# Clustered attention with two MLPs: late transposes ahead of score tiles, key penalties undivided, two roundings as SyncE copies, and a new order of the first units

## The chip, the cores and the metric

The kernel runs on one core of a Trainium2 chip. The metric is the time of one execution on the device in microseconds (us), as the median of several runs. The core's engines are TensorE (PE; its weight loads are listed apart as PEld), VectorE (DVE), ScalarE (ACT), GpSimd (POOL) and SyncE (SP), which in this kernel issues the DMAs.

## The reference

Eight heads of two batches attend within clusters: a query sees only the keys whose nearest centroid is its own. The result goes through two MLPs.

```python
q_assign = argmax(einsum('bhsd,hcd->bhsc', q_n, c_n))      # S = 768, D = 64, 16 clusters
k_assign = argmax(einsum('bhsd,hcd->bhsc', k_n, c_n))
mask = q_assign[:, :, :, None] == k_assign[:, :, None, :]
scores = where(mask, scale * q @ k.T, -1e9)
attn_out = softmax(scores) @ v                              # B = 2, H = 8
x = attn_out as (1536, 512)
h = maximum(maximum(x @ w1, x @ w2), x @ w3); x = h @ w_out         # d_ff = 768
h = x @ w_in; g = maximum(0.01 * h, h); out = g @ w_out             # d_ff = 2048
```

## The kernel before

**Work.** Heads go in eight pairs; a pair fills 128 partitions with 2 x 64 dimensions. A unit is one head of a pair and a group of 256 queries, so that a pair has six units and the attention 48 (n = 0 to 47). In the first pair the units are (0,0), (0,1), (1,0), (1,1), (0,2), (1,2) as (head, group); in later pairs an even unit is head 0 and an odd one head 1. Each value is kept as a rounded part and a rest (fp32r), which gives operands q1, q2, k1, k2 per head and for even and odd pairs: `k1_0_1` is k1 of even pairs, head 1. Sixteen rows of q2 and k2 hold one-hot clusters and penalties (`oo`), by which keys of other clusters fall out of the softmax.

**Operations of a unit n.** S0:n and S1:n are score tiles of 128 queries by 768 keys (PE, L659, four matmuls: a first half from q1 and k1, a second half from q2 and k2, which needs the penalties); SA and SB are these halves apart. M0, M1 are the maxima (VectorE, L665), X0, X1 the exponentials (ScalarE, L671, tile `ee`), R the inverse of their sums, Q0, Q1 the normalising (GpSimd, L685). T0, T2, T4 transpose two of six blocks of both halves (PE, L692, four transposes each); E0, E2, E4 bring them out of PSUM (L705, L707, tile `et`). V is the product with the values for two units (PE, L716, 24 matmuls), Y its store into `acc` (ScalarE, L722).

**Operations of a pair p.** G, C, H are the cluster similarities (L545, L553, L561), Na, Nb, W, FA, FB the one-hot of the first nearest cluster; O and P are its transposes (PE, L578) and the penalties (ScalarE, L583, tile `oo`). QH, QL, KH, KL round and take rests. D*@p copies operands into their places by SyncE's queue: Dq, Dk, Dl, Dm those of queries, keys and rests (64x768, 192 KB each), Da and Db the penalties of head 0 and of head 1 (four copies of 16x384, 24 KB). LD and LV load a pair's queries and keys (2 x 384 KB) and values. F fetches MLP weights (`raw` and `low`, some 512 KB each); I3 and I2 are idle matmuls on zeros (L836). The first pair has operations of its own: Gq, Gk, Naq to FBk as above for queries and keys apart, UQ and UK the transposes of the query and the key one-hots (L532), CQ and CK the query and key penalties out of PSUM, and Z.. the roundings of head a and b: `Zbr` fills q2 of head 1, `Zbj` the lower half of k1 of head 1 (ScalarE, L419), `Zbm` is GpSimd's rest for k2 of head 1, which reads that lower half. `Hd` is a small cast on GpSimd (`hold`), by which its work begins when the first one-hots are there.

**Order.** Each engine works through its instructions in the order of the program, and waits only for semaphores. That order is written out by hand: BEGIN lists the operations of units 0 to 14 and what goes with them, ORDER has one row for each of the six units of a pair (the number behind / or + is an offset in units or pairs) and serves the rest, and END ends the attention. ONCE names operations that are done once, ahead of a given one, and skipped where they would have come. What stands ahead of another on an engine, and on SyncE's queue, is read from these.

A piece of the operand copies, where Da and Db are:

```python
elif part == "ab"[j]:
    for b in range(4):
        rows = slice((2 * b + j) * C, (2 * b + j + 1) * C)
        cols = slice(b % 2 * HALF, (b % 2 + 1) * HALF)
        dma((q2, k2)[b // 2][D : D + C, cols], s["oo"][rows])
```

Of the kernel before, what the change touches and what calls it, by code (L numbers as in the profile page):

```python
# [8 lines left out]
F32 = mybir.dt.float32  # L9
F32R = mybir.dt.float32r  # L10
BF16 = mybir.dt.bfloat16
AF = mybir.ActivationFunctionType
# [34 lines left out]
)  # L47

BEGIN = (
    "Gq Zaq Zal Zak Naq Nbq Zaj Gk Wq Zbj FAq Zbq Nak SA0:0 FBq Zar Nbk I3 UQ Wk CQ FAk SA1:0 G@1 Zbk FBk UK  "  # L50
# [14 lines left out]
)  # L65
AFTER = 12

END = "h h V:47 h h Y:47"

ONCE = {  # L70
    "V:43": "in x0 x1 x2 x3", "T0:46": "ph h h", "T4:46": "h h", "T0:47": "h", "T4:47": "h h",
    "E4:47": "oh",
}
# [15 lines left out]
def clustered_attention_mlps(  # L89
# [229 lines left out]
    with ExitStack() as att:  # L319
# [302 lines left out]
        def first_operands(j, what):  # L622
            s = st[0]
            q1, q2, k1, k2 = opnd[0][j]
            rq, rk = (s[x][j * D : (j + 1) * D] for x in ("rq", "rk"))
            if what == "q":
                rounded("A", q1[0:D], rq, SCALE)
            elif what == "r":
                rounded("A", q2[0:D], rq, SCALE)
            elif what == "k":  # L630
                rounded("A", k1[0:D], rk)
            elif what == "j":
                rounded("A", k1[D:P], rk)
            elif what == "l":
                rest("D", q1[D:P], rq, q1[0:D], SCALE)
            else:
                rest("DP"[j], k2[0:D], rk, k1[j * D : (j + 1) * D])
# [91 lines left out]
        def scrap(key):  # L729
            if key not in scraps:  # L730
                scraps[key] = small_bank()
            return scraps[key]
# [82 lines left out]
        if True:  # L815
# [65 lines left out]
            def start(op):  # L881

                if op[0] == "I":
                    idle(int(op[1:]))
                elif op[0] == "Z":
                    first_operands("ab".index(op[1]), op[2])
                elif op == "Hd":

                    nc.gpsimd.tensor_copy(hold, oh0[:, D + 2 * C : D + 2 * C + 1])
                elif op == "Ct":  # L890
                    end_third()
                elif op == "D2":
                    operands(0, "2")
                elif op == "w":
                    take_apart()
                elif op in ("Gq", "Gk"):
                    sims(0, "qk".index(op[1]), scrap(op))
                elif op in ("Naq", "Nak"):
                    near_max(0, "qk".index(op[2]), scrap("G" + op[2]))
                elif op in ("Nbq", "Nbk"):  # L900
                    near_eq(0, "qk".index(op[2]))
                elif op in ("Wq", "Wk"):
                    weigh(0, nc.vector, "qk".index(op[1]))
                elif op in ("FAq", "FAk"):
                    first_max(0, "qk".index(op[2]))
                elif op in ("FBq", "FBk"):
                    first_eq(0, "qk".index(op[2]))
                elif op in ("UQ", "UK"):
                    onehot_up(0, "QK".index(op[1]), scrap(op))
                elif op == "CQ":  # L910
                    ps = scrap("UQ").bitcast(BF16)[D : D + C, 0:S]
                    nc.scalar.copy(opnd[0][0][1][D : D + C], ps)
                elif op in ("CK", "CL"):
                    up = slice(D, D + C)
                    cols = slice(0, HALF) if op == "CK" else slice(HALF, S)
                    ps, out_ = scrap("UK").bitcast(BF16)[up, cols], opnd[0][0][3][up, cols]
                    if op == "CK":
                        nc.scalar.activation(
                            out_, ps, AF.Identity, scale=gain[up], bias=base[up]
                        )  # L920
                    else:
                        nc.vector.tensor_scalar(
                            out_, ps, gain[up], base[up], op0=ALU.mult, op1=ALU.add
                        )
                elif op == "OT":
                    for h in range(2):
                        onehot_T(0, h, scrap(op)[:, 256 * h : 256 * h + 256])
                elif op == "PA":
                    penalties(0, scrap("OT"))
                elif op == "in":  # L930
                    until_scores.close()
                    open_inputs()
                elif op == "oh":
                    until_transposes.close()
                    open_hidden()
                elif op == "F":
                    fetch_pieces()
                elif op == "ph":
                    until_exps.close()
                    open_products()  # L940
                    st["first"] = hidden(0, 0)
                elif op == "h":
                    next(st["first"])
                elif op[0] == "x":
                    split_x(0, (int(op[1]),))
                else:
                    raise ValueError(op)
# [109 lines left out]
```

## Time and profile before

| | us |
|---|---|
| three runs | 695.46, 695.75, 698.95 |
| median | 695.75 |
| profiled execution, own time | 696.57 |
| its span | 694.8 |

The span runs from the first to the last instruction of the profiled execution; the own time holds some 1.8 us around it. In the rows below a group of instructions stands with its line, engine, operation and tile; "x4" is how many are taken together; what stands in square brackets is idle time of the engine just ahead and what ended it. Line numbers of the kernel after the change are one to five higher.

### The profile page before, as it was taken

The numbers are of one execution on the slowest core, as the hardware profiler recorded it, in microseconds if no ns is written. First come the engines' busy times: TensorE is split into PE (matmuls) and PEld (weight loads), VectorE is DVE, ScalarE is ACT, GpSimd is POOL, SyncE is SP. The second block draws the span as 40 slices with busy tenths as digits, with TensorE's granted clock in tenths as the row PEclk, the third lists the DMA queues.
The fourth block names the chain that finished last, engine by engine and source line by source line (L and its number), as shares of the span: only waits on it lengthen the run. The fifth ranks groups of instructions, "written<-read, shape, count | busy, mean of one in ns | idle before, by whom it ended". The sixth has DMA issues, their size and how long they took to land.

```text
span 694.8 us, 10351 instructions
## 1 busy us (share of the span) xinstructions
PE 684.9 (99%) x3715; PEld 551.0 (79%) x3717; DVE 489.0 (70%) x896; ACT 336.9 (48%) x635; POOL 217.7 (31%) x201
## 2 busy tenths in 40 slices
PE   8999999999999999999999999999999999999997
PEld 5677778777786788888888888888888888888886
DVE  6887788888867398788783798797359847972222
ACT  6877777877877354323231344454434324431120
POOL 4855456465544011011111102322322223312220
PEclk9999999999999999999999999999999999999999
DMA  3969748427401166545541344265215522500102
GB/s 120 235 153 268 196 112 242 136 74 200 101 13 50 51 204 204 173 157 162 169 161 52 121 152 152 62 204 189 91 54 188 166 77 91 182 30 1 57 34 91
DMA packets 30083, 89.96 MB, mean 129 GB/s; under 512 B 4785, under 2 KB 5681, under 8 KB 30033
## 3 DMA queue, kind: packets, MB, share of 16 engines
q1 hardware_dynamic: 30032, 89.32, 42.7%
q8 instruction: 29, 0.48, 0.3%
q14 instruction: 22, 0.17, 0.1%
HBM read 68.16 MB, written 3.15 MB: 103 GB/s over the span
## 4 chain that ended last, share of the span: by engine, by line
PE 94%; DMA 2%; POOL 1%; DVE 1%; ACT 1%; issue 0%; SPq 0%; ACTq 0%; POOLq 0%
PE h L246 13%; PE h L247 13%; PE h L248 13%; PE o L716 9%; PE s L659 9%; PE y L246 9%; PE y L248 9%; PE y L247 9%; PE t L692 8%; DMA k<-kh 1%; PE s L836 1%; DMA k<-oo 1%; PE t L545 1%; DVE xl L237 1%; ACT ee L671 0%; PE t L465 0%
## 5 line engine op out<-in xcount | busy, mean ns | idle before, releaser
L280 POOL TENSOR_TENSOR hl<-a,hh 128x512 fp32r<-128x512 f32 x66 | 92.0, 1394 | 355.5 <-ACT hh L279 355.5
L246 PE MATMUL h<-xh,wh 128*128 128x512 f32 x408 | 159.3, 390 | 0.0
L248 PE MATMUL h<-xh,wl 128*128 128x512 f32 x408 | 158.8, 389 | 0.0
L247 PE MATMUL h<-xl,wh 128*128 128x512 f32 x408 | 158.7, 389 | 0.0
L665 DVE TENSOR_REDUCE mx<-s 128x1 f32<-128x768 f32 x96 | 90.8, 954 | 36.1 <-PE s L659 27.5
L685 POOL TENSOR_SCALAR ee<-ee,rs 128x768 f32<-128x768 f32 x96 | 90.5, 956 | 62.0 <-DVE rs L680 34.9
L246 PE MATMUL y<-hh,wh 128*128 128x512 f32 x264 | 102.7, 389 | 0.0
L247 PE MATMUL y<-hl,wh 128*128 128x512 f32 x264 | 102.7, 389 | 0.0
L248 PE MATMUL y<-hh,wl 128*128 128x512 f32 x264 | 102.7, 389 | 0.0
L279 ACT CAST hh<-a 128x512 fp32r<-128x512 f32 x66 | 41.1, 623 | 126.3 <-DVE a L273 75.4
L659 PE MATMUL s<-k,q 128*128 128x512 f32 (+3 forms) x384 | 93.0, 363 | 3.2 <-ACT ee L671 1.6
L671 ACT ACTIVATE ee<-s,mx 128x768 f32<-128x768 f32 x96 | 86.8, 905 | 19.1 <-DVE mx L665 15.3
L246 PEld LDWEIGHTS h<-xh,wh 128*128 128x128 f32 x408 | 76.6, 188 | 16.5 <-issue 0.8
L248 PEld LDWEIGHTS h<-xh,wl 128*128 128x128 f32 x408 | 76.6, 188 | 16.0
L247 PEld LDWEIGHTS h<-xl,wh 128*128 128x128 f32 x408 | 76.6, 188 | 15.6
L271 ACT COPY a<-h 128x512 f32<-128x512 f32 x66 | 38.7, 586 | 96.0 <-PE h L248 94.5
L692 PE MATMUL t<-idf,ee 128*128 128x128 f32 x576 | 78.5, 274 | 0.6 <-POOL ee L685 0.3
L306 DVE TENSOR_TENSOR acc<-y,acc 128x512 f32<-128x512 f32 x72 | 48.6, 686 | 40.5 <-PE y L248 40.5
L275 DVE SCALAR_TENSOR_TENSOR a<-a,h 128x512 f32<-128x512 f32 x48 | 32.9, 685 | 61.7 <-ACT a L271 61.6
L659 PEld LDWEIGHTS s<-k,q 80*128 80x128 f32 (+1 forms) x384 | 58.8, 191 | 19.1 <-ACT ee L671 7.9
L692 PEld LDWEIGHTS t<-idf,ee 128*128 128x128 f32 x576 | 65.8, 141 | 8.6 <-issue 2.1
L705 ACT COPY et<-t 128x512 f32<-128x512 f32 x96 | 55.2, 587 | 27.8 <-PE t L692 27.3
(107 smaller groups left out, 840.6 us busy)
## 6 DMA issues: line engine op xcount, KB each, us to landing
raw<-in_w SPq DMA_DIRECT2D x56, 512.0 KB, 4.1
low<-in_w SPq DMA_DIRECT2D x56, 511.5 KB, 3.5
q<-qh SPq DMA_DIRECT2D x28, 192.0 KB, 4.8
k<-kh SPq DMA_DIRECT2D x28, 192.0 KB, 5.4
rq<-in_qT SPq DMA_DIRECT2D x8, 384.0 KB, 3.5
rk<-in_kT SPq DMA_DIRECT2D x8, 384.0 KB, 4.1
rv<-in_v SPq DMA_DIRECT2D x8, 384.0 KB, 4.9
out_T<-acc SPq DMA_DIRECT2D x12, 256.0 KB, 2.0
```

What stands on the lines that cost most here:

```text
L246: nc.tensor.matmul(ps, ah, bh, start=(k == 0), stop=False)
L247: nc.tensor.matmul(ps, ah, bl, start=False, stop=False)
L248: nc.tensor.matmul(ps, al, bh, start=False, stop=(k == n - 1))
L280: nc.gpsimd.tensor_tensor(hlo[:, f, :], a, hh[:, f, :].bitcast(F32), op=ALU.subtract)
L306: nc.vector.tensor_tensor(a, ps, a, op=ALU.add)
L659: nc.tensor.matmul(ps[:, lo:hi], a[:, c0 : c0 + P], b[:, lo:hi], start=start, stop=not start)
L665: nc.vector.tensor_reduce(mx, un[n]["s", i], axis=AX.X, op=ALU.max, negate=True)
L671: nc.scalar.activation(e, u.pop(("s", i)), AF.Exp, bias=u.pop(("m", i)), scale=1.0, accum_out=u["sum"][:, i, 0:1],)
L685: nc.gpsimd.tensor_scalar(e, e, un[n]["rs"][:, i : i + 1], 1.0, op0=ALU.mult, op1=ALU.mult)
L692: nc.tensor.transpose(ps[:, kk, i * P : (i + 1) * P], u["e"][i][:, (k + kk) * P : (k + kk + 1) * P], idf,)
L705: nc.scalar.copy(out, ps)
L716: nc.tensor.matmul(un[n]["o"][j * D : (j + 1) * D], v[:, t, j, :], done[p, g, j][:, t, :], start=(t == 0), stop=(t == NQ - 1),)
```

## The change

BEGIN is written in another order. ONCE gains three entries: T4:36 and T0:37 are done ahead of S0:40, T4:42 and T0:43 ahead of S0:46, and the store Y:41 ahead of the exponential X1:47. The key penalties of the first pair (CK) are one ScalarE instruction over 768 columns; before, ScalarE and VectorE (CL) did a half each. Zbr and Zbj for head 1 become copies on SyncE's queue of what ScalarE has already rounded into q1 and k1.

```diff
 BEGIN = (
-    "Gq Zaq Zal Zak Naq Nbq Zaj Gk Wq Zbj FAq Zbq Nak SA0:0 FBq Zar Nbk I3 UQ Wk CQ FAk SA1:0 G@1 Zbk FBk UK  "
...
+    "Zaq Gq Zal Naq Zar Gk Nbq Zak Wq FAq FBq Zbq Nak Nbk UQ Zbk Zaj Wk FAk G@1 FBk CQ UK C@1 Hd QH@1 Zam  "
...
 ONCE = {
+    "S0:40": "T4:36 T0:37", "S0:46": "T4:42 T0:43", "X1:47": "Y:41",
...
             if what == "q":
                 rounded("A", q1[0:D], rq, SCALE)
+            elif what == "r" and j == 1:
+                nc.sync.dma_start(out=q2[0:D].bitcast(F32), in_=q1[0:D].bitcast(F32))
             elif what == "r":
                 rounded("A", q2[0:D], rq, SCALE)
             elif what == "k":
                 rounded("A", k1[0:D], rk)
+            elif what == "j" and j == 1:
+                nc.sync.dma_start(out=k1[D:P].bitcast(F32), in_=k1[0:D].bitcast(F32))
             elif what == "j":
                 rounded("A", k1[D:P], rk)
...
-                elif op in ("CK", "CL"):
+                elif op == "CK":
+                    ps = scrap("UK").bitcast(BF16)[D : D + C, 0:S]
                     up = slice(D, D + C)
-                    cols = slice(0, HALF) if op == "CK" else slice(HALF, S)
-                    ps, out_ = scrap("UK").bitcast(BF16)[up, cols], opnd[0][0][3][up, cols]
-                    if op == "CK":
-                        nc.scalar.activation(
-                            out_, ps, AF.Identity, scale=gain[up], bias=base[up]
-                        )
-                    else:
-                        nc.vector.tensor_scalar(
-                            out_, ps, gain[up], base[up], op0=ALU.mult, op1=ALU.add
-                        )
+                    nc.scalar.activation(
+                        opnd[0][0][3][up], ps, AF.Identity, scale=gain[up], bias=base[up]
+                    )
```

**PE at the start.** Before, behind the similarities of queries and keys (L465) stand the first half of the first score tile (L659), three idle matmuls on `nought` (L836) and then UQ, the transposes of the query one-hots `oh` (L532):

```order
L465 MATMUL t1_129<-cb_106,rq0_107 128x32 x6
L465 MATMUL t0_128<-cb_106,rk0_108 128x32 x6
L659 MATMUL s0_126<-k1_0_0_133,q1_0_0_131 128x512
L659 MATMUL s0_126<-k1_0_0_133,q1_0_0_131 128x256
L836 LDWEIGHTS nought_161
L836 MATMUL s2_130<-nought_161 128x512
...
L532 LDWEIGHTS oh0_206
L532 MATMUL t1_129<-idb_103,oh0_206 80x128
```

After, UQ (L533) follows the similarities at once, and then come the similarities of pair 1 (L546) and UK, and only behind them the first halves of the score tiles:

```order
L466 MATMUL t1_129<-cb_106,rq0_107 128x32 x6
L466 MATMUL t0_128<-cb_106,rk0_108 128x32 x6
L533 LDWEIGHTS oh0_206
L533 MATMUL t1_129<-idb_103,oh0_206 80x128
...
L546 MATMUL t0_128<-rq1_109,cb_106 32x384 x2
L546 MATMUL t0_128<-rk1_110,cb_106 32x384 x2
L533 LDWEIGHTS oh0_206
L533 MATMUL t1_129<-idb_103,oh0_206 80x128
...
L664 MATMUL s0_126<-k1_0_0_133,q1_0_0_131 128x512
L664 MATMUL s0_126<-k1_0_0_133,q1_0_0_131 128x256
```

The score tile's half moved behind UQ and UK, and the idle matmuls of this place are gone; in all there are six fewer at the start.

**SyncE's queue for pair 2.** Before, the copies of the penalties `oo2` to head 1 (`q2_0_1`, `k2_0_1`) and head 0 (`q2_0_0`, `k2_0_0`) stand ahead of key copies and of the weight fetches F; the loads LD@4 (`rq`, `rk` from L412) follow F:

```order
L598 DMA q2_0_1_136<-oo2_633 16x384 x2
L598 DMA k2_0_1_138<-oo2_633 16x384 x2
L598 DMA q2_0_0_132<-oo2_633 16x384 x2
L598 DMA k2_0_0_134<-oo2_633 16x384 x2
L598 DMA k2_0_0_134<-kl2_733 64x768
L598 DMA k2_0_1_138<-kl2_733 64x768
L598 DMA k1_0_0_133<-kh2_484 64x768 x2
L598 DMA k1_0_1_137<-kh2_484 64x768 x2
L142 DMA raw0_0_868<-in_w 128x2048
L142 DMA low0_0_870<-in_w 128x2046
L142 DMA raw0_1_872<-in_w 128x2048
L142 DMA low0_1_874<-in_w 128x2046
```

After, LD@4 and F stand between the copies to head 0 and those to head 1:

```order
L413 DMA rv1_112<-in_v 128x768
L599 DMA q2_0_0_132<-oo2_732 16x384 x2
L599 DMA k2_0_0_134<-oo2_732 16x384 x2
L413 DMA rq0_107<-in_qT 128x768
L413 DMA rk0_108<-in_kT 128x768
L143 DMA raw0_0_815<-in_w 128x2048
L143 DMA low0_0_817<-in_w 128x2046
L143 DMA raw0_1_819<-in_w 128x2048
L143 DMA low0_1_821<-in_w 128x2046
L599 DMA q2_0_1_136<-oo2_732 16x384 x2
L599 DMA k2_0_1_138<-oo2_732 16x384 x2
L413 DMA rv2_113<-in_v 128x768
```

Head 1's four copies moved from the place ahead of the weights to the one behind them; unit 13 (S0:13) is the first to read them.

**PE at unit 40.** Before, S0:40 (four matmuls into bank s0 from `k1_0_0` to `q2_0_0`) stands ahead of T4:36 and T0:37:

```order
L659 MATMUL s0_126<-k1_0_0_133,q1_0_0_131 128x512
L659 MATMUL s0_126<-k1_0_0_133,q1_0_0_131 128x256
L659 MATMUL s0_126<-k2_0_0_134,q2_0_0_132 128x512
L659 MATMUL s0_126<-k2_0_0_134,q2_0_0_132 128x256
L692 MATMUL t2_405<-idf_102,ee0_114 128x128
L692 MATMUL t2_405<-idf_102,ee1_115 128x128
...
L692 MATMUL t0_128<-idf_102,ee2_116 128x128
L692 MATMUL t0_128<-idf_102,ee3_117 128x128
```

After, these two groups of four transposes stand ahead of it, and S1:40 (bank s1) follows at once:

```order
L697 MATMUL t2_393<-idf_102,ee0_114 128x128
L697 MATMUL t2_393<-idf_102,ee1_115 128x128
...
L697 MATMUL t0_128<-idf_102,ee2_116 128x128
L697 MATMUL t0_128<-idf_102,ee3_117 128x128
...
L664 MATMUL s0_126<-k1_0_0_133,q1_0_0_131 128x512
L664 MATMUL s0_126<-k1_0_0_133,q1_0_0_131 128x256
L664 MATMUL s0_126<-k2_0_0_134,q2_0_0_132 128x512
L664 MATMUL s0_126<-k2_0_0_134,q2_0_0_132 128x256
L664 MATMUL s1_127<-k1_0_0_133,q1_0_0_131 128x512
```

The score tile moved behind eight transposes; at unit 46 it is the same.

## Rows read from the trace of the kernel before

**Rows 1.** Page, busy us, share of the span and instructions by engine.
```profile
PE 684.9 (99%) x3715; PEld 551.0 (79%) x3717; DVE 489.0 (70%) x896; ACT 336.9 (48%) x635; POOL 217.7 (31%) x201
```

**Rows 2.** Waits of PE: us in total, times, longest.
```profile
PE s L659 <- ACT ee L671: 1.6, 3, 0.6
...
PE s L659 <- DMA k<-oo: 0.8, 1, 0.8
...
PE o L716 <- ACT acc L722: 0.6, 1, 0.6
```

**Rows 3.** Timeline, 9 to 26 us: start, us, engine, operation [idle before <-releaser].
```profile
9.55 0.19 PEld L532 LDWEIGHTS <-oh 128*80 128x80 bf16 x1 [0.28 <-DVE e L496]
...
10.86 0.36 DVE L516 TENSOR_TENSOR oh<-e,m 128x192 bf16<-128x192 f32 x1 [0.99 <-PE t L532]
...
11.29 0.84 POOL L889 CAST hold<-oh 128x1 f32<-128x1 bf16 x1 [7.80 <-DVE oh L516]
...
13.58 0.66 ACT L918 ACTIVATE k<-t,lines 16x384 fp32r<-16x384 bf16 x1 [0.57 <-DVE k L922]
...
14.27 0.99 ACT L590 ACTIVATE oo<-t,lines 64x768 fp32r<-64x768 bf16 x1
...
25.79 0.31 PEld L692 LDWEIGHTS t<-idf,ee 128*128 128x128 f32 x3 [0.49 <-POOL ee L685]
```

**Rows 4.** Chain that ended last, 23 to 40 us: start, us, what.
```profile
23.16 6.64 DMA k<-kh
...
34.47 0.33 PE t L561 x3
34.80 2.74 PE o L716 x24
37.54 0.89 PE s L659 x4
38.43 0.44 PE t L692 x4
38.87 0.71 PE s L659 x4
```

**Rows 5.** Timeline, PE, ACT and SyncE's issues (SPq), 1 to 62 us.
```profile
1.17 0.42 SPq L412 DMA_DIRECT2D rq<-in_qT  x1
...
3.06 0.43 SPq L412 DMA_DIRECT2D rv<-in_v  x1
...
42.67 0.17 PEld L578 LDWEIGHTS <-oh 128*128 128x128 bf16 x3 [0.16 <-issue]
...
43.68 0.67 ACT L583 ACTIVATE oo<-s,lines 128x384 fp32r<-128x384 bf16 x1
...
53.53 0.59 SPq L142 DMA_DIRECT2D raw<-in_w  x1
...
58.70 2.46 SPq L598 DMA_DIRECT2D q<-qh  x4
```

**Rows 6.** DMA issues of four moments: KB each, us from issue to landing.
```profile
rq<-in_qT SPq DMA_DIRECT2D x1, 384.0 KB, 3.2
...
rv<-in_v SPq DMA_DIRECT2D x1, 384.0 KB, 6.1
...
q<-oo SPq DMA_DIRECT2D x2, 24.0 KB, 1.8
...
q<-qh SPq DMA_DIRECT2D x1, 192.0 KB, 10.3
```

**Rows 7.** Timeline, units 40 and 41, and the end of attention.
```profile
183.99 0.97 PE L659 MATMUL s<-k,q 128*128 128x512 f32 x4 [0.62 <-ACT ee L671]
...
186.12 0.90 ACT L671 ACTIVATE ee<-s,mx 128x768 f32<-128x768 f32 x1
...
187.18 0.96 PE L659 MATMUL s<-k,q 128*128 128x512 f32 x4
...
226.54 0.66 PE L692 MATMUL t<-idf,ee 128*128 128x128 f32 x4 [0.28 <-DVE et L707]
```

28 rows, old and new, of the table BEGIN are left out of this document.

## Prediction

> **What bounds the kernel now.** I read the page's table of engines first. TensorE (PE) is busy 684.9 of 694.8 us, 99%, and the next, VectorE, 70% [rows 1]. No engine can take a large piece off this time; what a change can win is PE's idle time, about 10 us in all, and idle matmuls that only fill it. Where that idle time lies is in the list of what PE waited for [rows 2]: 1.6 us in three waits for the exponentials `ee`, 0.8 for the copy of head penalties (`k<-oo`), 0.6 for a store of `acc`. So I worked in steps of a few tenths of a microsecond, at four places: the start (to some 35 us), the copies through SyncE's queue at 43 to 70 us, units 40 and 46, and the last store. A gain of PE at any place is kept only as far as no later wait takes it back.
>
> **Place 1, the start: a gain.** Before, PE runs the first score tile's half (SA0:0) and three idle matmuls ahead of the query one-hots' transposes (UQ). UQ's first weights load at 9.55. The key one-hots (FBk, VectorE, written into the same tile) wait 0.99 us for UQ's reads and start at 10.86, so GpSimd's `hold` starts at 11.29 [rows 3]. After, UQ stands ahead of SA0:0 and the idle matmuls of that place are gone. FBk can then start when the operation ahead of it on VectorE ends, which is 10.86 - 0.99 = 9.87; with a tenth for issue, 0.9 us earlier. From `hold` to the transposes of unit 1 at 25.79, which waited for GpSimd (0.49 on the weight load) [rows 3], GpSimd runs the same 12 pieces in both programs, only in another order. So those transposes come at 25.79 - 0.9 = 24.9.
>
> From there to the first values (V:2) the new order puts on PE eight groups of transposes (0.44 each), five score tiles (0.70 each, of the rows 0.71) [rows 4] and some small pieces: the other three transposes of the group at 24.9 (0.33), three of H@2 (0.33 in the row `t L561`) and two idle matmuls, which I set at 0.44. That is 3.52 + 3.50 + 1.10 = 8.12; I add 0.4, somewhat less than one more wait for an exponential (1.6 in three, [rows 2]). V:2 starts at 33.4 in place of 34.80 [rows 4], 1.4 earlier, and PE then has one score tile and one group of transposes more behind it: 0.70 + 0.44 = 1.14. Together 2.5 us. Not all of it stays. The copy of penalties for S0:6, for which PE waited 0.8 before [rows 2], comes only 0.9 to 1.3 earlier, with all that it depends on, while PE wants it some 2.3 earlier; so the wait grows by 1.0 to 1.4 at most, or by less where V:2 and other work can go ahead of it. I take 0.7. **Term 1: -2.5 + 0.7 = -1.8** (bounds -2.5 and -1.2).
>
> Two ScalarE roundings (Zbr, Zbj) become SyncE copies of 192 KB. The trace has no such copy at this moment. From below: 1.8 us to landing, as 24 KB took with little ahead of it [rows 6]; from above 6.64, the piece of the chain for `k<-kh`, 192 KB each with others around it [rows 4]. The copy of keys is issued when Zbk ends, about 8.7, while the first loads still land (the last was issued at 3.06 and took 6.1) [rows 5, 6]; I take 2.5, near the lower end, since only some 0.5 us of those loads is left then. It lands at 11.3, and GpSimd wants it after `hold` (0.84) and one rounding (0.83), near 12.1. So nothing. At 6.64 it would land at 15.3, 3.2 late for GpSimd, and term 1 would shrink to nothing or turn to a loss of about 1 us; I leave that end to the range.
>
> Undivided key penalties: before, ScalarE's half (0.66) began only 0.57 after it could, because VectorE's half on the same tile went first [rows 3]. Together that is 1.23 from transposes to the end. One piece of 768 columns took 0.99 [rows 3]. It isn't slower, is 0.24 shorter, and is not the last thing that PE waits for any more; I count 0, and VectorE is rid of its half.
>
> **Place 2, a new wait: a loss.** This is in SyncE's queue. Before, the eight small copies of pair 2's penalties (Da@2, Db@2) were issued ahead of the weight fetch F and of the loads LD@4. After, Db@2's four stand behind LD@4 (2 x 384 KB) and F (2 x 512 and 2 x 511.5 KB), 2815 KB in all, and the second half of S0:13 reads what they bring (unit 13 is head 1 of pair 2). The unit of time here is t0, the start of the penalties P@2 on ScalarE. It was at 43.68, 1.0 after PE's O@2 (42.67) [rows 5].
>
> When PE wants it: between O@2 and that half the new order has 0.17 of O@2, nine groups of transposes (3.96), five score tiles (3.55), two units of values (2 x 2.74 = 5.48), 0.2 more for each of the two tiles behind values (0.89 against 0.71), and the tile's first half (half of 0.71) [rows 4]: 13.9 after O@2, or t0 + 12.9.
>
> When it lands: P@2 takes 0.67 [rows 5], then four copies of head 0 at some 0.6 an issue (a single issue took 0.59), so LD@4 goes out at t0 + 3.2. If only issues counted, the rest (two loads, four fetches, four copies) would be out by t0 + 10 and land 1.8 later [rows 6]: t0 + 11.8, no wait. But bytes count too. The first loads show the rate with nothing else going: the first was issued at 1.17 and took 3.2, the last at 3.06 and 6.1 [rows 5, 6]; between the two landings, 4.37 and 9.16, four loads of 384 KB arrived, 321 KB a us. Then LD@4's first lands at t0 + 6.4, the other 2431 KB need 7.6, and the small copies follow at about t0 + 14.3: a wait of 1.4. From above there is a row of this very sequence: `q<-qh`, issued at 58.70 behind F and LD, took 10.3 [rows 5, 6], so it landed at 69.0, which is 15.5 after F's first issue at 53.53. That gives t0 + 18.7 and a wait of 5.8, but there 768 KB of key copies lay ahead in the queue, which at 321 KB a us is 2.4 of it: 3.4. Between 1.4 and 3.4 I take the middle. **Term 2: +2.5** (bounds 0 and 5.8).
>
> The Trainium skill, page "DMA: Bandwidth & Descriptors", section "Where 436 GB/s comes from", says that for transfers between HBM and SBUF the HBM side binds, at about 358 GB/s per core. At that figure 2431 KB would need some 6.9 us instead of 7.6, an estimate from the page, and the wait would be 0.7 shorter; the trace's 321 is lower, and I use the trace's. The same page's section on queues, rings and completion order states that each DMA engine consumes its descriptors in ring order, which speaks against this change, since small copies can't overtake; the 10.3 us of `q<-qh` agrees.
>
> **Place 3, units 40 and 46: nothing, or a little worse.** PE waited 0.62 at S0:40 for an exponential [rows 7]. After, eight transposes (T4:36, T0:37; 2 x 0.44) run ahead of it. They fill the wait, but are longer than it: S0:40 starts 0.88 - 0.62 = 0.26 later. It is not PE's order that limits here but a cycle: S0:40, its maximum, its exponential (186.12 + 0.90), S0:41 at 187.18 in the same bank [rows 7]. That is 3.19 from tile to tile, and PE's work between them shrinks by the 0.88 that was moved. So the wait goes from S0:40 to S0:41 or a little further, and the cycle ends up to 0.26 later. **Term 3: +0.1 for each of the two places, +0.2** (bounds 0 and +0.5; -1.2 is a rival).
>
> **Place 4, Y:41 ahead of X1:47: 0.** The store frees the accumulator for V:43, which waited 0.6 for it [rows 2]. V:43 starts some 0.6 earlier, but the next transposes waited for VectorE's `et` (0.28, at 226.54) [rows 7], which stands behind the splitting of the inputs on ScalarE and VectorE, and ScalarE has the same work in sum. The wait moves there. X1:47 starts 0.36 later, under those.
>
> **Sum:** -1.8 + 2.5 + 0.2 + 0 = +0.9. The profiled execution took 696.57 with its span of 694.8; the median of the runs shown is 695.75, so the profile is 0.8 above it and typical. On the median: **696.7 us**, no change by a bound of 0.5% (3.5 us), which is about what a measurement of this kernel can tell from no change.
>
> **The rivals.**
> *A, no wait at S0:13.* The issue order would not matter because all lands by t0 + 12.9. For it: the sum by issues alone. Against: 2815 KB at 321 a us. Then only terms 1 and 3 count: -1.6, 694.1 us.
> *B, slower.* The wait at S0:13 is as long as the row of 10.3 us says, 5.8, or term 1 is lost to a late key copy. One mechanism: Db@2 behind F. 5.8 - 1.8 + 0.2 = +4.2 gives 700.0. It decides for slower from a wait of 5.1 (3.5 + 1.8 - 0.2). For it: the same queue with the same 2.8 MB. Against: the key copies that lay ahead there and aren't here.
> *C, faster.* PE's waits at 40 and 46 really vanish (2 x 0.62 = 1.2), V:43's too (0.6), the start keeps its 2.5, and no wait comes at S0:13: -4.3, 691.4 us. For it: PE is 99% busy, so that each wait gone should count. Against: each of these waits stands in a cycle that another engine closes.
>
> **How the numbers follow.** My forecast (a wait of 1 to 4 us, the sum between -1 and +3) gets 0.62, A 0.17, B 0.13, C 0.08. A and the forecast lie within 0.5% and B and C outside: same 0.79, which I round to 0.78 for a large term 1; slower 0.14, since term 1 can also be lost to the key copy; faster 0.08. For 8 in 10 the range leaves out C and the far half of B: from 693.5 (A with 0.6 more of term 1) to 700.3 (B, with term 3 at its upper end). The forecast's own range is 694.8 to 698.8.
>
> **What would show it.** Right: `hold` near 10.4 in place of 11.29; V:2 near 33.4; a wait of PE for DMA `q<-oo` or `k<-oo` of 1 to 4 us at S0:13, near 55, with Db@2's issue behind F; no wait of 0.62 at S0:40, but one of like size at the next tile or two; PE's busy time about 1 to 2 us smaller for the idle matmuls that are gone. Wrong: no DMA wait near 55 (A, and the sum is negative); a GpSimd wait for `k` near 12 (the copy late); waits at 40, 46 and V:43 gone with nothing in their place (C); or a span that moves with none of these.

## The result, and the profile after

The change took 701.23 us in the median of six runs (700.69 to 702.86) against 695.57 (695.2 to 698.95, six runs): slower by 0.77%, ratio 1.0077 with a 95% interval of 1.0058 to 1.0096. The forecast was 696.7 and its range ended at 700.3. The profiled execution is the fastest of the six (700.69; span 698.9).

The page of the change, its line of engines and its line of the chain by engine:

```profile
PE 685.8 (98%) x3711; PEld 552.8 (79%) x3711; DVE 489.5 (70%) x895; ACT 335.0 (48%) x633; POOL 220.1 (31%) x201
...
PE 91%; DVE 3%; DMA 2%; SPq 1%; issue 1%; ACT 1%; ACTq 0%; DVEq 0%
```

PE is as busy as before [rows 1], but the DMA waits and ScalarE, VectorE and issue ahead of them have come into the chain. PE's busy time did not fall by the 1 to 2 us that the prediction named as a sign, though six idle matmuls are gone. What PE waited for, in the change (us in total, times, longest):

```profile
PE s L664 <- DMA k<-oo: 4.6, 2, 4.0
...
PE s L664 <- ACT ee L676: 1.4, 6, 0.4
```

Where [rows 2] had one wait of 0.8 for the copies of penalties there are two with 4.6 together, and one of them has 3.99. The timeline of the change, from several stretches: UQ, FBk and `hold` at the start, FB@1 and KL@1, the first values, then penalties P@2, SyncE's issues (SPq), the values ahead of S0:13, its two halves and the next values.

```profile
8.99 0.86 PE L533 MATMUL t<-idb,oh 128*80 128x128 bf16 x6 [0.67 <-DVE oh L517]
...
10.49 0.36 DVE L517 TENSOR_TENSOR oh<-e,m 128x192 bf16<-128x192 f32 x1
...
10.91 0.84 POOL L894 CAST hold<-oh 128x1 f32<-128x1 bf16 x1 [7.40 <-DVE oh L517]
...
22.25 2.28 DVE L517 TENSOR_TENSOR oh<-e,m_None 128x384 bf16<-128x384 f32 x1
...
22.29 1.82 POOL L431 TENSOR_TENSOR kl<-rk,kh 128x768 fp32r<-128x768 f32 x1
...
35.71 2.81 PE L721 MATMUL o<-et,rv 128*64 128x256 f32 x24
...
52.52 0.68 ACT L584 ACTIVATE oo<-s,lines 128x384 fp32r<-128x384 bf16 x1
...
56.80 0.58 SPq L413 DMA_DIRECT2D rq<-in_qT  x1
...
60.04 1.69 SPq L599 DMA_DIRECT2D q<-oo  x2
...
62.55 2.81 PE L721 MATMUL o<-et,rv 128*64 128x256 f32 x24
...
65.29 0.61 PE L664 MATMUL s<-k,q 128*128 128x512 f32 x2
...
69.90 0.60 PE L664 MATMUL s<-k,q 80*128 80x512 f32 x2 [3.99 <-DMA k<-oo]
...
76.50 2.81 PE L721 MATMUL o<-et,rv 128*64 128x256 f32 x24
```

P@2 starts at 52.52, LD@4 is issued at 56.80, Db@2 behind the weights at 60.04, and PE, done with the first half of S0:13 at 65.9, stands until 69.90. The start is no better: `hold` comes at 10.91 (11.29 in [rows 3]), 0.4 earlier and not 0.9, and FB@1 takes 2.28. What followed on the long wait is in the stretches of the change (from and to, length in us; busy time of PE, PEld, DVE, ACT and POOL with the number of instructions; granted clock of TensorE as a share of full speed; DMA share, GB/s):

```profile
9.00:10.00 1.00, 1.00 (x10) 0.83 (x14) 0.93 (x3) 0.10 (x1) 0.00 (x0) 0.50 0.68 160
...
66.00:68.00 2.00, 0.00 (x0) 0.00 (x0) 0.00 (x0) 0.00 (x0) 0.89 (x2) 1.00 1.07 313
...
70.00:72.00 2.00, 2.00 (x9) 1.86 (x10) 0.96 (x1) 0.55 (x2) 0.00 (x0) 0.59 1.04 214
72.00:74.00 2.00, 2.00 (x11) 1.90 (x11) 1.25 (x2) 1.13 (x4) 0.00 (x0) 0.56 1.03 220
74.00:76.00 2.00, 2.00 (x17) 1.88 (x15) 1.17 (x4) 1.54 (x4) 1.24 (x2) 1.00 1.06 269
```

PE did nothing from 66 to 68 and next to nothing to 70, and behind that the granted clock was 0.59 and 0.56 for four microseconds, which means mostly the lower of its two levels (1.2 in place of 2.4 GHz). At the start it was 0.50 from 9 to some 12 us, after PE had waited 0.67 for the first one-hots. The profile of before, from which the prediction took its rows, has the same: 0.50 from about 8 to 11 us, with PE busy all that time.

From stretch to stretch of PE's values, the difference to before grows to 5.6 us by 87 us (86.96 against 81.33), and falls by 1.0 between the values near 200 and the first MLP matmul (28.31 us in the change, 29.31 before); another 0.3 goes near 150 us, and I did not follow that. So there are three places to explain: S0:13 (a loss), the late moves (a gain of 1.0, which I had at -0.2), the start (about 0, which I had at 1.8). In the trace PE's first values come at 35.71 against 34.80 [rows 4], and the score tile and the group of transposes that the prediction priced at 1.14 are done by then.

### The profile page after: what moved, and what is told of

It reads as the page before. It is cut to its first block, busy times and chain, and to the rows that moved or that the text cites. A ratio compares the mean times of both kernels' runs of the same rounds, so it can differ in the third digit from the quotient of the medians.

```text
span 698.9 us, 10343 instructions
## 1 busy us (share of the span) xinstructions
PE 685.8 (98%) x3711; PEld 552.8 (79%) x3711; DVE 489.5 (70%) x895; ACT 335.0 (48%) x633; POOL 220.1 (31%) x201
## 4 chain that ended last, share of the span: by engine, by line
PE 91%; DVE 3%; DMA 2%; SPq 1%; issue 1%; ACT 1%; ACTq 0%; DVEq 0%
PE h L247 13%; PE h L249 13%; PE h L248 13%; PE y L248 9%; PE y L249 9%; PE y L247 9%; PE s L664 8%; PE o L721 8%; PE t L697 7%; DMA k<-oo 2%; DVE mx L670 2%; SPq L599 1%; PE t L546 1%; PE s L841 1%; DVE xl L238 0%
## 5 line engine op out<-in xcount | busy, mean ns | idle before, releaser
L690 POOL TENSOR_SCALAR ee<-ee,rs 128x768 f32<-128x768 f32 x96 | 92.4, 975 | 70.8 <-DVE rs L685 40.0
```

The lines of the kernel that those rows point to most:

```text
L690: nc.gpsimd.tensor_scalar(e, e, un[n]["rs"][:, i : i + 1], 1.0, op0=ALU.mult, op1=ALU.mult)
```

## The experiments

Each ran beside the kernel before on the same chip; medians of 8 to 12 runs, the ratio to before with its 95% interval. My theory after the result: the four copies Db@2 behind 2815 KB are the loss, by the wait and by the clock behind it. The rivals are named in each expectation.

**Db@2 ahead of the weights.** On the change:

```diff
- X1:10 T0:8 E2:7 Da@2 QH@3
+ X1:10 T0:8 E2:7 Da@2 Db@2 QH@3
...
- Q0:10 S1:12 Db@2 E2:9
+ Q0:10 S1:12 E2:9
```

> The change with one edit: the four copies of pair 2's penalties to head 1 (Db@2) are issued right behind those to head 0, ahead of the loads LD@4 and the weight fetches F. Theory (the wait at S0:13 is these copies behind 2815 KB, and the slow clock behind it is the price of PE's standing still): the wait of 3.99 us is gone, the granted clock stays at 1.00 from 60 to 80 us, and 5.7 us are won against the change: 695.5 us, or 0.0 against before. Rival 1 (the wait only moves to the next copies in the queue, those of qh and kh for pair 3, which now come behind): a wait of 2 us or more for q or k later than 70 us, 698 to 700. Rival 2 (only the wait is won, the clock falls anyway, at some later gap): 697.2.

695.27 us, 0.9997 (0.9985 to 1.0009). From 60 to 80 us PE had no idle time:

```profile
60.00:80.00 20.00, 20.00 (x154) 15.68 (x153) 15.35 (x29) 15.97 (x33) 12.93 (x13) 1.00 1.00 277
```

The values ahead of S0:13 and the next ones, in this kernel:

```profile
61.85 2.81 PE L721 MATMUL o<-et,rv 128*64 128x256 f32 x24
...
69.99 2.81 PE L721 MATMUL o<-et,rv 128*64 128x256 f32 x24
```

The whole loss hangs on the place of four copies of 24 KB: 5.96 us in the medians, 5.6 by the ratios. No later copy took the wait over.

**Only the weights behind Db@2.** The loads stay ahead of it:

```diff
- E0:8 T0:9 F X0:11
+ E0:8 T0:9 X0:11
...
- Q0:10 S1:12 Db@2 E2:9
+ Q0:10 S1:12 Db@2 F E2:9
```

> The change with one edit: the weight fetches F (2047 KB) go behind Db@2; the loads LD@4 (768 KB) stay ahead of it. Theory (bytes ahead in the queue set the wait): in the change 2815 KB issued from 56.80 had Db@2 land at 69.9, 13.1 us, so 768 KB need some 4 to 5 us from 56.80 and land near 62, before PE wants them at 65.9: no wait, 695.5, as with Db@2 ahead of everything. Rival (what lay late was the issue of LD@4 itself, 4.4 after the start of the penalties, and not the bytes of F): a wait of 2 us or more remains, 698 to 700.

694.98, 0.9995 (0.9984 to 1.0006), no DMA wait. 768 KB ahead of the copies cost nothing; the 2047 KB of F decide.

**Idle matmuls in the wait.** On the change, between the halves of S0:13; J18 is 18 idle matmuls into a bank of their own:

```diff
- V:7 E0:9 Q1:10 S0:13 X1:12
+ V:7 E0:9 Q1:10 SA0:13 J18 SB0:13 X1:12
```

> The change (Db@2 still behind the weights) with 18 idle matmuls between the two halves of S0:13, into a bank of their own. In full clock they take 18 x 0.21 = 3.8 us of a wait of 3.99. Theory (the loss at S0:13 has two parts, 4.0 of standing still and 1.7 of slow clock after it, since the granted clock was 0.59 and 0.56 from 70 to 74 us): the copies land no earlier, but the clock stays at 1.00 behind them, and 1.7 us are won against the change: 699.5. Rival (the clock falls for another reason than PE's idle time, or its fall costs nothing because other waits cover it): 701.2 or more, the idle matmuls adding what overhangs the wait.

699.08, 1.0044 (1.0025 to 1.0063), 2.15 less than the change. The stretches of this kernel:

```profile
66.00:68.00 2.00, 2.00 (x10) 0.92 (x10) 0.00 (x0) 0.00 (x0) 0.63 (x1) 1.00 1.08 292
...
70.00:72.00 2.00, 2.00 (x19) 1.92 (x18) 1.80 (x2) 1.52 (x3) 0.00 (x0) 1.00 1.06 212
72.00:74.00 2.00, 2.00 (x16) 1.77 (x14) 1.75 (x5) 1.80 (x5) 0.83 (x1) 1.00 1.02 240
```

Its values ahead of S0:13, the second half of S0:13 and the next values:

```profile
62.30 2.81 PE L721 MATMUL o<-et,rv 128*64 128x256 f32 x24
...
69.21 0.70 PE L664 MATMUL s<-k,q 80*128 80x512 f32 x2
...
74.34 2.81 PE L721 MATMUL o<-et,rv 128*64 128x256 f32 x24
```

With PE busy over the time of the wait the clock stays at 1.00. From the values ahead of S0:13 to the next ones it took 12.04 us (62.30 to 74.34), in the change 13.95, with Db@2 ahead 8.14. So 5.8 were lost here, and the idle matmuls gave 1.9 of it back. Not all of the 1.9 is the clock: in this run the second half of S0:13 began 6.91 after those values, in the change 7.35, so 0.4 is a shorter wait. Behind it the way to the next values took 5.13 against 6.60. The slow clock cost about 1.5, and the waiting the rest.

**The late moves.** On the kernel before, in ONCE: the first line alone, the second alone, and both:

```diff
+    "S0:40": "T4:36 T0:37", "S0:46": "T4:42 T0:43",
+    "X1:47": "Y:41",
```

> The kernel before with only the four groups of transposes ahead of S0:40 and S0:46. My prediction: the wait of 0.62 moves to a later tile, +0.1 each, 695.8 (+0.2 against before). Theory after the change's trace (offset of PE against before fell from 5.28 at the values of unit 43 to 4.28 at the first matmul of the MLPs, and the waits of 0.62 are 0 there, with 0.17 and 0.18 left a tile later): the waits do go, 0.4 to 0.5 us won at each place or 1.0 in all: 694.6.

> The kernel before with only the store Y:41 ahead of the exponential X1:47. My prediction: the wait of 0.58 for acc moves to et at 226.54, 0 won: 695.6. Rival: the wait goes, 0.6 won: 695.0. The profile decides by whether the transposes behind the first MLP matmuls wait longer than 0.28 for et.

> The kernel before with all three entries of ONCE (transposes ahead of S0:40 and S0:46, the store ahead of X1:47) and the old start. From the stretches of the traces: the values at 194.88 to the first MLP matmul take 29.31 before, 29.30 with the transposes alone, 28.66 with the store alone, 28.31 in the change. Theory: the store is worth 0.65 and the transposes nothing by themselves: 694.7 to 694.9. Rival: the two together are worth the 1.0 of the change: 694.3 to 694.5, the stretch 28.3.

The transposes alone: 695.52, 1.0012 (0.9994 to 1.003). The store alone: 694.57, 0.9981 (0.9967 to 0.9996). All: 694.60, 0.9989 (0.997 to 1.0008). The timeline of PE with the transposes alone, the two tiles behind S0:46 that wait, and V:43:

```profile
210.23 0.96 PE L660 MATMUL s<-k,q 128*128 128x512 f32 x4 [0.17 <-ACT ee L672]
...
212.62 0.96 PE L660 MATMUL s<-k,q 128*128 128x512 f32 x4 [0.55 <-ACT ee L672]
...
219.68 2.81 PE L717 MATMUL o<-et,rv 128*64 128x256 f32 x24 [0.57 <-ACT acc L723]
```

The wait of 0.62 at S0:46 became 0.17 and 0.55 at the next two tiles: nothing won, as predicted. V:43 still waits 0.57 for `acc`. With the store alone, S0:46 and V:43:

```profile
209.72 0.97 PE L660 MATMUL s<-k,q 128*128 128x512 f32 x4 [0.62 <-ACT ee L672]
...
219.68 2.81 PE L717 MATMUL o<-et,rv 128*64 128x256 f32 x24
```

V:43 does not wait, and the wait for `et`, where I had put this gain's end, is gone too. By the stretch from the values near 195 to the first MLP matmul the store is worth 0.65 (28.66 against 29.31). All three on the old start take 28.66 as well, so the 0.35 that the change has more needs its other BEGIN too. It lies at S0:46: from the values ahead of it to the next ones 10.38 us (208.97 to 219.35), 10.73 before and with the transposes alone; the second of the two waits is 0.18 there in place of 0.55. Why stays open.

**UQ first, without the idle matmuls.** My first step by itself, on the kernel before:

```diff
- FAq Zbq Nak SA0:0 FBq Zar Nbk I3 UQ Wk CQ
+ FAq Zbq Nak FBq UQ SA0:0 Zar Nbk Wk CQ
```

> The kernel before with one edit at the start: UQ goes ahead of SA0:0 and the three idle matmuls of that place go. My prediction's first step by itself: FBk starts near 9.9 in place of 10.86 and hold near 10.4 in place of 11.29, GpSimd's chain and the first values come 0.9 earlier than 34.73, and 694.7 against 695.5 of before. Rival (PE without the idle matmuls runs the start at the lower clock, granted 0.50, and the gain is eaten): hold no more than 0.4 earlier, the time within 0.3 of before.

697.45, 1.0019 (1.0004 to 1.0034). Its timeline and its stretches:

```profile
8.85 0.86 PE L532 MATMUL t<-idb,oh 128*80 128x128 bf16 x6 [0.76 <-DVE oh L516]
...
9.95 0.36 DVE L516 TENSOR_TENSOR oh<-e,m 128x192 bf16<-128x192 f32 x1
...
10.38 0.84 POOL L889 CAST hold<-oh 128x1 f32<-128x1 bf16 x1 [6.80 <-DVE oh L516]
...
35.42 2.81 PE L716 MATMUL o<-et,rv 128*64 128x256 f32 x24
```

```profile
7.00:8.00 1.00, 1.00 (x10) 0.95 (x9) 0.90 (x4) 0.98 (x2) 0.00 (x0) 0.93 1.02 412
8.00:9.00 1.00, 0.24 (x3) 0.15 (x3) 1.00 (x4) 0.96 (x3) 0.00 (x0) 0.50 0.34 135
...
13.00:14.00 1.00, 0.78 (x5) 0.28 (x3) 0.56 (x1) 0.11 (x1) 0.92 (x2) 0.50 0.00 0
```

FBk and `hold` come just when the prediction has them, 9.95 and 10.38, and yet the first values come at 35.42 against 34.80. The clock was 0.50 from just before 8 us to 14 us; PE was idle for most of the stretch from 8 to 9, but the clock fell a little ahead of that wait. The mean granted clock of a whole run tells how often: its median is 0.999 in 123 runs of before, 0.997 in 12 of this one and 0.993 in the 6 of the change (which holds the slow microseconds behind S0:13 too); 0.002 of 695 us is 1.4. Among the 12 runs of this kernel the eight with a mean clock below 0.999 have a median of 697.6, and three of the other four took 694.6 to 695.5.

**UQ first, idle matmuls kept.** As above, with I3 ahead of UQ:

```diff
- FAq Zbq Nak SA0:0 FBq Zar Nbk I3 UQ Wk CQ
+ FAq Zbq Nak FBq I3 UQ SA0:0 Zar Nbk Wk CQ
```

> The kernel before with UQ ahead of SA0:0, but the three idle matmuls kept, now ahead of UQ. Without them this order took 697.45, its granted clock was 0.50 from 8 to 14 us, and hold came at 10.38. Theory (clock): most runs have a mean clock of 0.999 or 1.0 again, hold stays near 10.4, and the time is 694.7 to 695.2. Rival (the order itself is slower, since SA0:0 now stands in front of work that UK needs): 697 with the clock at 0.999.

695.86, 1.0006 (0.9989 to 1.0022); the median clock is 0.999 again. The idle matmuls give back 1.6 us by the medians and 0.9 by the ratios, whose intervals overlap; the earlier UQ brings nothing. That holds at the full clock too: the eight runs with a mean clock of 0.999 or more have a median of 695.57, those of before beside them 695.25. So the step "GpSimd 0.9 earlier, so all 0.9 earlier" fails in this order. The profile can't say why, since its clock was 0.50 from about 10 to 13 us; PE's waits for exponentials are 3.0 us in five there, 1.6 in three in [rows 2].

**KL@1 behind Q1:1.** On the kernel with Db@2 ahead:

```diff
- Ct T2:0 KL@1 Dq@1
+ Ct T2:0 Dq@1
...
- X1:3 Q1:1 Dk@1
+ X1:3 Q1:1 KL@1 Dk@1
```

> The kernel with Db@2 ahead of the weights and one edit more: GpSimd's rest of the keys of pair 1 (KL@1) goes behind Q1:1. Theory (the missing gain at the start is a meeting of two engines: VectorE's FB@1, 0.67 elsewhere, took 2.22 there, as long as GpSimd's KL@1 beside it, and O@1, the sims' copy and the maxima waited behind it): FB@1 takes about 0.7, the first values come 1 us earlier than 34.99, and the time is 694.3 against 695.3. Rival (the start's end is set elsewhere, by the exponentials or the copies of penalties to S0:6): FB@1 is short but the first values come within 0.3 of 34.99, and 695.3 stays.

694.53, 0.9985 (0.9972 to 0.9999), with a median clock of 0.997; the interval overlaps that of the kernel that it is made from, so that it alone doesn't decide.

**Idle matmuls ahead of UQ** on the last, and in a second kernel **ahead of UK too** (the lower pair of lines):

```diff
- Nak Nbk UQ Zbk
+ Nak Nbk I3 UQ Zbk
...
- FBk CQ UK C@1
+ FBk CQ I2 UK C@1
```

> The kernel with Db@2 ahead of the weights and KL@1 behind Q1:1, and now three idle matmuls ahead of UQ, where PE waited 0.67 for VectorE's first one-hots. Theory (the change's start lost its gain to the clock: its runs have a mean granted clock of 0.995 to 0.997 where those of before have 0.999, and the profiles show 0.50 from 9 to some 12 us or longer in every run of the new start): with PE kept busy the clock stays at 1.00 in most runs, the mean clock is 0.999, and 1.5 to 2 us are won on 694.5: 692.5 to 693. Rival (the clock falls whatever PE does there, or the idle matmuls delay UQ as much as they save): mean clock 0.997, 694.5 or more.

> As the run before, with two more idle matmuls ahead of UK, where PE waits for the key one-hots. Theory: if the first three don't hold the clock, these do, and 692.5 results; if the first three are enough, no difference between the two within 0.4. Rival: idle matmuls in front of UK delay it and the key penalties, 693.5 to 695.

The first: 693.93, 0.9966 (0.9951 to 0.9982), median clock 1.00. The second: 694.80, 0.999 (0.9972 to 1.0008), clock 0.999: no better, and with more runs that are longer for a reason that I didn't follow. Stretches and timeline of the first:

```profile
8.00:9.00 1.00, 0.97 (x9) 0.47 (x7) 0.93 (x4) 0.98 (x2) 0.00 (x0) 1.00 0.29 114
9.00:10.00 1.00, 0.87 (x11) 0.16 (x8) 0.93 (x3) 0.98 (x2) 0.00 (x0) 1.00 0.42 95
```

```profile
10.11 0.36 DVE L517 TENSOR_TENSOR oh<-e,m 128x192 bf16<-128x192 f32 x1
...
10.54 0.84 POOL L894 CAST hold<-oh 128x1 f32<-128x1 bf16 x1 [7.06 <-DVE oh L517]
...
21.66 0.67 DVE L517 TENSOR_TENSOR oh<-e,m_None 128x384 bf16<-128x384 f32 x1
...
23.07 1.84 POOL L431 TENSOR_TENSOR kl<-rk,kh 128x768 fp32r<-128x768 f32 x1
...
33.44 2.81 PE L721 MATMUL o<-et,rv 128*64 128x256 f32 x24
```

The clock is held, `hold` comes at 10.54, FB@1 takes 0.67 apart from KL@1, and the first values come at 33.44, the number that the prediction had (33.4). It had reached it from rows of a slow clock, though; what the old start does at the full clock is shown under term 1 below.

**KL@1's share.** The same with KL@1 where the change has it, and the kernel of 693.93 once more, on one chip:

```diff
- Ct T2:0 Dq@1
+ Ct T2:0 KL@1 Dq@1
...
- X1:3 Q1:1 KL@1 Dk@1
+ X1:3 Q1:1 Dk@1
```

> The kernel with Db@2 ahead of the weights and three idle matmuls ahead of UQ, but KL@1 where the change has it, beside FB@1. Together with KL@1 moved this took 693.93. Theory (both count at the start): the clock is held, FB@1 takes about 2 us beside KL@1, and the time is 694.6 to 694.9, 0.7 to 1.0 slower than with KL@1 moved. Rival (the clock alone held the gain): within 0.3 of the run beside it.

> The same kernel as the one with three idle matmuls ahead of UQ and KL@1 behind Q1:1 (693.93, ratio 0.9966), beside the run without KL@1's move on the same chip: 693.5 to 694.2 again.

With KL@1 early 694.14, 0.9979 (0.9964 to 0.9994); with it late 693.77, 0.9966 (0.995 to 0.9983). In the first, FB@1 and KL@1:

```profile
24.53 2.29 DVE L517 TENSOR_TENSOR oh<-e,m_None 128x384 bf16<-128x384 f32 x1
...
24.58 1.83 POOL L431 TENSOR_TENSOR kl<-rk,kh 128x768 fp32r<-128x768 f32 x1
```

Again FB@1 takes 2.29 beside it. From `hold` to the first values this trace has 23.96 us (13.18 to 37.14), that of the kernel at 693.93 has 22.90. But the times differ by 0.4 only (0.0013 in ratio) with overlapping intervals: that the two meet is shown, that it costs time at the end is not. The second profile of the better kernel has FB@1 at 0.64, but 0.50 of clock from about 8.4 to 11.8 us, and its first values come at 35.65: the idle matmuls ahead of UQ don't hold the clock in every run.

**The roundings on ScalarE again,** on the kernel with Db@2 ahead: the two branches of the change with the copies are left out.

```diff
-            elif what == "r" and j == 1:
-                nc.sync.dma_start(out=q2[0:D].bitcast(F32), in_=q1[0:D].bitcast(F32))
...
-            elif what == "j" and j == 1:
-                nc.sync.dma_start(out=k1[D:P].bitcast(F32), in_=k1[0:D].bitcast(F32))
```

> The kernel with Db@2 ahead of the weights, with Zbr and Zbj as ScalarE roundings again, as before (two instructions of 0.84 on ScalarE, no copies). My prediction counted the copies at nothing, hidden in the wait for GpSimd: 695.3, no difference. Rival (ScalarE is behind at this place: the key penalties and the first exponentials come 0.84 to 1.7 later): 696 to 697, and then the copies were worth about 1 us.

695.19, 0.9985 (0.997 to 0.9999), against 695.27: the SyncE copies are hidden and worth nothing that these times show, as predicted.

## Why the prediction was wrong

Two terms of its sum failed: term 2 was +2.5 and S0:13 lost 5.8, and term 1 was -1.8 where the change's start won nothing.

**Term 2, the new wait: right mechanism, wrong size.** The prediction's place, cause and order were right: Db@2 behind LD@4 and F, wanted by S0:13's second half. It had LD@4 at t0 + 3.2, the want at t0 + 12.9 and the landing at t0 + 15.4; with t0 = 52.52 the trace shows 4.3, 13.4 and 17.4. Against the sum at 321 KB a us (landing at t0 + 14.3) three pieces of about 1 us each were short. Head 0's four copies took SyncE 3.5 us to issue and not 2.4. From the landing of LD@4's first load (59.9) to that of the last weight piece (68.6) it took 8.7, not 7.6. And the small copies were there 1.3 behind that piece, not 0.3. From LD@4's issue to the landing it took 13.1 us. The row of the same sequence, 15.5 less the 2.4 of the key copies, had said just this; the rate of the first loads, 321 KB a us, gave 11.1. Where two bounds came from a like transfer and from an unlike one, I took their middle. The DMA landings of the change (one issue each, KB, us):

```profile
low<-in_w SPq DMA_DIRECT2D x1, 511.5 KB, 9.3
...
q<-oo SPq DMA_DIRECT2D x1, 24.0 KB, 8.9
```

The small copy took 8.9 where 24 KB with little ahead took 1.8 [rows 6]; it did not overtake the weights (68.9, behind 68.6).

**A term that was missing: the clock.** Behind 3.99 us of standing still PE worked at a granted clock of 0.59 and 0.56 for 4 us, which cost about 1.5. The sum counted a wait at its own length. So +2.5 was 5.8, and rival B's bound of 5.1 was passed by this part. The Trainium skill ("TensorE: Matmul & The Clock Gate", Part 1, "What's actually happening") says that a hardware block sets the array's clock by how busy PE has been of late; the trace agrees here, with 1.00 in the run that kept PE busy over the same microseconds; at the start it does so only in part, as the last section says.

**Term 1, the start: its first step rested on rows of a slow clock.** I had read the profile of before as typical, 0.8 above the median. Its mean clock of 0.997 is that of 21 among 123 runs of before, where the median is 0.999, and the wait of 0.99 that FBk had for UQ [rows 3] lies in its slow microseconds. The first line here is a stretch of that profile; the others are from the old start at the full clock (the profile with all three late moves): the same stretch, FBk, `hold` and the first values.

```profile
9.00:10.00 1.00, 1.00 (x4) 0.37 (x3) 0.80 (x3) 0.98 (x2) 0.00 (x0) 0.50 0.00 0
...
9.00:10.00 1.00, 1.00 (x12) 0.71 (x10) 0.93 (x3) 0.99 (x2) 0.00 (x0) 1.00 0.02 9
...
10.14 0.36 DVE L517 TENSOR_TENSOR oh<-e,m 128x192 bf16<-128x192 f32 x1
...
10.57 0.84 POOL L890 CAST hold<-oh 128x1 f32<-128x1 bf16 x1 [7.04 <-DVE oh L517]
...
33.23 2.81 PE L717 MATMUL o<-et,rv 128*64 128x256 f32 x24
```

In the old order at the full clock, too, FBk does not wait for UQ, and `hold` comes at 10.57, as in the new order with the clock held (10.54). The start of a run shifts by some tenths, so the surer measure is from VectorE's first one-hots to `hold`: 2.82 us in the profile of before, 1.93 to 1.98 in the three profiles of the old start at the full clock, 1.93 with UQ ahead of SA0:0, 2.33 in the order of the change. So the 0.9 was what the slow clock had cost in that one profile, not what UQ's place was worth; that `hold` came at 10.38 and 10.54 where the prediction had it near 10.4 is luck. In the change FBk came at 10.49: the granted clock was 0.50 from some point between 8.7 and 10.2 us on, for some 3 us or longer, in all six profiles that have the change's start without idle matmuls ahead of UQ. The prediction counted the idle matmuls as work that only fills idle time; with three of them put back the clock was held more often. And "the same 12 pieces on GpSimd, only in another order" left out who runs beside them: FB@1 took 2.28 beside KL@1. With both mended, the profile at the full clock is ahead of the old start's by 0.97 at the values near 86 us (86.04 against 87.01). The times of the two kernels, measured beside each other (693.93 and 694.60; 0.9966 and 0.9989), differ by 0.7 in the medians and 1.6 in the ratios, with overlapping intervals, and that holds what the new order wins later. So the start is worth about 1 us in place of 1.8, and by which of its moves stays open.

**Term 3** was right for the moves by themselves: the wait at S0:46 moved to the next two tiles and nothing came of it. In the change 0.35 came at S0:46, with a cause that is open. **Term 4** was wrong by 0.65: the wait for `et` behind V:43 did not take the gain; with V:43 earlier nothing waits there.

So the 5.66 between the medians divide into 5.96 at S0:13 (701.23 against 695.27), some -0.9 for the late moves (694.60 against 695.52) and what is left, +0.6, for the start. These are differences of medians from several chips, on which before itself had 695.34 to 696.02, so the last is not clear of the noise.

## What to carry to other kernels

Look at what stands ahead of a small copy in its queue, in bytes, whenever a list of operations is reordered: 2 MB of prefetch that nobody needed yet, put ahead of four copies of 24 KB each that PE waited for, cost 6 us of 695. Price a wait of PE by its length and by the clock behind it, and idle matmuls by the clock that they may hold, not by the idle time that they fill. Look at the granted clock of the stretch before rows of it go into a sum. When two bounds come from a like and an unlike case, take the like one.

The best version, faster than both kernels: the change with Db@2 ahead of the weights, three idle matmuls ahead of UQ and KL@1 behind Q1:1, 693.93 and 693.77 us in two sets of runs (0.9966 of before in both).

## What the runs showed of the hardware

A VectorE operation with two operands in SBUF beside a GpSimd operation with two: FB@1 took 2.28 and 2.29 us where it began 0.04 and 0.05 us ahead of KL@1, and ended 0.42 and 0.41 after it; in the kernel at 693.93, where it ended before KL@1 began, it took 0.67, while KL@1 took 1.82 to 1.84 in these three. The Trainium skill ("SBUF — State Buffer", "Summary: rules for kernel authors") says that VectorE with two SBUF inputs and a GpSimd operation that reads SBUF exclude each other, and that the second to issue waits for the first. The trace agrees that one holds up the other; but here VectorE's was recorded as the first, and was still the one held up. In four more profiles it began 0.04 to 0.31 after KL@1, took 1.94 to 2.22 and ended 0.42 after it too. Where FB@1 began some 0.6 ahead (the kernel with idle matmuls ahead of UQ and UK), it took 1.06 and KL@1 2.12.

A PE that waited 0.67 us at 8.3 us was followed by a granted clock of 0.50 for 3 us or more; with three idle matmuls in that time the mean clock of a run was 0.999 or 1.00 in 24 of 35 runs (three sets), without them in 5 of 44 (the four kernels with Db@2 ahead of the weights). The idle matmuls make the slow clock rarer and don't rule it out. Three profiles with idle matmuls ahead of UQ (before, the one with more ahead of UK, and the second of the better kernel) have 0.50 for some 3 us from about 8 us on, with PE busy throughout, and the wait came after the fall where UQ was first on the old start. What else decides it is not shown.
